# Block 0's second products as single fp32 matmuls, w_out's split parts made for block 1, and a dense slot for weight values

## The chip, the cores and the metric

One core of a Trainium2 chip. TensorE (PE) multiplies, VectorE (DVE), ScalarE (ACT) and GpSimd (POOL) work elementwise, and SyncE (SP) and the other engines issue DMAs. Each engine has its own queue of instructions in a fixed order, and waits on semaphores for the others. The metric is the device time of one execution in microseconds (us), the median of several runs.

## The reference, cut to what matters

Windowed attention, then a first MoE layer (512 to 2048 to 512) on 2304 tokens, then a second one with a softmax-like gate and a layer norm. The change touches the first MoE layer:

```python
def _moe_ref(x, w_in, w_out):
    h = x @ w_in
    g = np.where(h >= 1, h, np.where(h <= -1, 0.0, (h + 1) ** 2 / 4))
    return (g @ w_out).astype(np.float32)
```

The weights lie in memory as 64-bit floats. The result has to be close to that of fp32.

## The kernel before, in words

**Precision.** A product is made of three fp32r matmuls: an fp32 value is cut into a high part, which fp32r holds exactly, and the low rest, and the kernel adds high x high, high x low and low x high. `wih`/`wil` are the parts of w_in, `woh`/`wol` those of w_out, `xh`/`xl` those of the attention's output, `gh`/`gl` those of the activation g.

**Weights.** w_in and w_out come in 16 units of 512 KB each (a unit is one chunk f of 128 of the 2048 inner columns), w_in f and w_out f by turns. A unit lands as pairs of 32-bit words in a staging buffer `st` (`wst`, NST of them in a ring), SP issues the load (L124, L126). `split_a` on ACT (L132) and `split_b` on DVE (L136, L137) turn the pair into an fp32 value in place, every second word of the buffer; `split_c` casts it to the high part on ACT (L145) and subtracts on POOL for the low part (L146). The buffer is free for the next load after that subtraction.

**Blocks and chunks.** The tokens go in 6 blocks of 384. For each block the 16 chunks pass through: `moe_h` (L496), 4 x 3 matmuls into a PSUM bank `ps_h`, of which there are two in block 0; `moe_g`, ACT's Relu and Square (L505, L506); `moe_g2`, DVE's `u` (L511), which reads the bank a last time and so releases it, and ACT's cast `gh` (L512); `moe_g3`, the subtraction `gl` (L516), on POOL in block 0 and on DVE later; and, two steps on, `moe_y` (L527), 4 x 3 matmuls into the four accumulators `acc`. The first two chunks of block 0 are worked on in halves of 192 tokens, the rest in whole 384.

**What lies between.** Attention work for the next tokens runs in slots between the chunks (`ps_s`, L352, scores; `p`, L360 to L386, softmax; `ps_p`, L400 and L402, transposes; `pT`; `ps_x`, L421, values), all in plain fp32 on PE. In block 0 the weight units are loaded and split as well, two per chunk; from block 1 on the second layer's weights follow at a slower pace.

**Order.** The code is written in steps (the loop over `seq`), but a scheduler settles the order in each engine's queue, by its own estimate of when each instruction could start; it may bring an instruction far ahead of the step at which it is written.

Of the kernel before, what the change touches and what calls it, by code (L numbers as in the profile page):

```python
# [20 lines left out]
def kernel(  # L21
# [23 lines left out]
    NB = 384  # L45
    TPJ = NB // TT
    NBLK = NT // NB
    NF = DFF // 128
    KC = DM // 128
    NG = NTILES * NP  # L50
    NST = 5
    G0, F0, NC, NQ, NV = 6, 2, 4, 6, 7
    GB = TPJ * NP * 2
    PU = GB // 2 + 1
# [7 lines left out]
    gl_sb = const.tile([128, DF2 // 128], F32, name="gl_sb")  # L62
# [19 lines left out]
    wk_p = ctx.enter_context(tc.tile_pool(name="wk", bufs=2))  # L82
    w_p = ctx.enter_context(tc.tile_pool(name="w", bufs=1))
# [25 lines left out]
    def as_f32(a):  # L109
        return a.bitcast(F32)  # L110
# [7 lines left out]

    wdma = []

    def w_unit(src, hi, lo, gain=None, eng=nc.sync):
        st = stage["p"].tile([128, 512, 2], U32, tag="st", bufs=NST, name="wst")
        if src.shape[0] == 128 and len(src.shape) == 3:
            w_dma = eng.dma_start(out=st.rearrange("p (k f) t -> p k (f t)", k=src.shape[1]), in_=src)  # L124
        else:
            w_dma = eng.dma_start(out=st.rearrange("p f t -> p (f t)"), in_=src)  # L126
        wdma.append(w_dma.ins)
        return st, hi, lo, gain

    def split_a(st, *_):  # L130
        val = st[:, :, 1].bitcast(F32)
        nc.scalar.activation(val, val, ACTF.Prelu, scale=2.0 ** -112, alpha=2.0 ** 32)  # L132

    def split_b(st, *_):
        low, high = st[:, :, 0], st[:, :, 1]
        nc.vector.tensor_scalar(low, low, 29, None, op0=ALU.logical_shift_right)  # L136
        nc.vector.scalar_tensor_tensor(  # L137
            high, high, 3, low, op0=ALU.logical_shift_left, op1=ALU.bitwise_or
        )

    def split_c(st, hi, lo, gain):
        val = st[:, :, 1].bitcast(F32)
        if gain is not None:
            nc.scalar.activation(val, val, ACTF.Copy, scale=gain)
        nc.scalar.copy(hi, val)  # L145
        nc.gpsimd.tensor_tensor(lo, val, as_f32(hi), op=ALU.subtract)  # L146

    w_raw, w_a, w_b = [], [], []

    def w_conv(start=True):  # L150
        if w_b:
            split_c(*w_b.pop(0))
        if w_a:
            w_b.append(w_a.pop(0))
            split_b(*w_b[-1])
        if w_raw and start:
            w_a.append(w_raw.pop(0))
            split_a(*w_a[-1])

    wih, wil, woh, wol = {}, {}, {}, {}  # L160

    def wtile(tag):
        return w_p.tile([128, 512], F32R, tag=tag, name=tag)

    def w1_unit(f, which):
        if which == 0:
            hi, lo = wtile(f"wih{f}"), wtile(f"wil{f}")
            wih[f] = hi.rearrange("p (k f) -> p k f", k=KC)
            wil[f] = lo.rearrange("p (k f) -> p k f", k=KC)
            src = w_in[:, f * 256:(f + 1) * 256].rearrange("(k p) f -> p k f", p=128)  # L170
        else:
            hi, lo = woh[f], wol[f] = wtile(f"woh{f}"), wtile(f"wol{f}")
            src = w_out[f * 128:(f + 1) * 128, :]
        return w_unit(src, hi, lo)

# [6 lines left out]
    def w2_unit(n, which):  # L182
        if which == 0:
            kc, a = divmod(n, 2)
            src = w_in2[kc * 128:(kc + 1) * 128, a * 1024:(a + 1) * 1024]
            return w_unit(src, None, None, None, nc.gpsimd)
        src = w_out2.rearrange("(b k i) m -> k b i m", b=4, i=32)[n]
        return w_unit(src, None, None, gl_sb[:, n:n + 1], nc.gpsimd)

# [3 lines left out]
    w2_units = {}  # L193
    W2STEPS = [F0 + NF + 15 * u // 4 for u in range(16)]

    def w2_step(n, act, dve):
        for age, do in ((0, None), (4, split_a), (5, split_b), (6, split_c)):
            if n - age not in W2STEPS:
                continue
            u = W2STEPS.index(n - age)  # L200
            if age == 0:
                w2_units[u] = w2_unit(u % 8, u // 8)
                continue
            with tc.issue_after(act), tc.issue_after(dve):
                if age < 6:
                    do(*w2_units[u])
                    continue
                st, _, _, gain = w2_units.pop(u)
                if u < 8:
                    z = stage["p"].tile([128, 512], F32, tag="st", bufs=NST, name="w2st")  # L210
                    nc.scalar.copy(z, st[:, :, 1].bitcast(F32))
                    nc.gpsimd.dma_start(out=w2d[u], in_=z)
                    continue
                z = stage["p"].tile([128, 2, 512], F32R, tag="st", bufs=NST, name="w2st")
                do(st, z[:, 0, :], z[:, 1, :], gain)
                nc.gpsimd.dma_start(out=w2d[u], in_=as_f32(z.rearrange("p t f -> p (t f)")))
# [270 lines left out]
    hps, gh, gl, acc = {}, {}, {}, {}  # L487
# [12 lines left out]
    def moe_g(part, ps):  # L500
        c = part[2]
        u = wk_p.tile([128, NB], F32, tag="u", name="u")[:, c]
        hi = wk_p.tile([128, NB], F32R, tag="gh", bufs=3, name="gh")[:, c]
        lo = wk_p.tile([128, NB], F32R, tag="gl", bufs=3, name="gl")[:, c]
        nc.scalar.activation(u, ps, ACTF.Relu, bias=half, scale=0.5)  # L505
        nc.scalar.activation(u, u, ACTF.Square)  # L506
        gh[part[0], part[1], part[2].start], gl[part[0], part[1], part[2].start] = hi, lo
        return ps, u, hi, lo

    def moe_g2(ps, u, hi, lo):  # L510
        g = nc.vector.scalar_tensor_tensor(u, u, 1.0, ps, op0=ALU.min, op1=ALU.max)  # L511
# [205 lines left out]
    u = {}  # L717
# [122 lines left out]

    ps2 = []

    P_STEPS = {8: "P1", 9: "P6", 10: "P7", 12: "P5", 14: "P4"}

    na = 32 - 4 * G0
    seq = [(0, f, c) for c in (FIRST, SECOND) for f in range(F0)]
    seq += [(j, f, WHOLE) for j in range(NBLK) for f in range(F0 if j == 0 else 0, NF)]
    for n in range(len(seq) + 2):
        if n < len(seq):
            j, f, c = seq[n]  # L850
            last = j == NBLK - 1
# [133 lines left out]
```

## Time and profile before

| | |
|---|---|
| median of 3 runs | 712.16 us (713.34, 710.51, 712.16) |
| profiled execution, its own time | 712.67 us |
| its span | 710.9 us |
| granted clock, mean | 0.993 |
| busy: PE, DVE, ACT, POOL | 685.6, 434.3, 413.0, 195.3 us |
| DMA, mean rate over the span | 125 GB/s |

A busy time counts an instruction from its start to its modelled end; matmuls overlap, so PE's cost per matmul is read from one start to the next. Block 0's whole chunks run from about 52 to 139 us of the span, and POOL's work lies for the most part in the first fifth of it.

### The profile page before, as it was taken

Reading aid. Unit: us, or ns where it says so; the run is one execution under the profiler, and the core shown is the slowest. Engines: PE = TensorE matmul, PEld = TensorE weight load, DVE = VectorE, ACT = ScalarE, POOL = GpSimd, SP = SyncE. Lnnn points to the kernel's source line nnn. Section 1 sums busy time; section 2 is a strip of 40 time slices with the busy share of each in tenths; the row PEclk is TensorE's granted clock in tenths of the full one; section 3 lists DMA queues with packets and bytes.
Section 4 is the critical chain, followed back from the end, with each engine's and each line's share of the span. In section 5 each row is a group of like instructions: output and inputs, shape, how many; then the busy total and the mean of one; then the engine's idle time right before and its main releaser. Section 6 shows DMA issues by size and latency. Waiting matters only on the chain.

```text
span 710.9 us, 12663 instructions
## 1 busy us (share of the span) xinstructions
PE 685.6 (96%) x4439; PEld 630.0 (89%) x4439; DVE 434.3 (61%) x1147; ACT 413.0 (58%) x1006; POOL 195.3 (27%) x217
## 2 busy tenths in 40 slices
PE   6899978999999999999999999999999899999998
PEld 5689768999999999999999999999988678888887
DVE  4549898555555555454455543642379799988850
ACT  5778886565566655565566665454455635545541
POOL 2358876200001000021112111652472223300000
PEclk9989999999999999999999999999999999999999
DMA  9986897534353623346352211452033554553321
GB/s 193 216 231 171 220 260 189 107 81 107 71 110 88 139 61 73 78 124 130 87 112 70 95 60 47 154 200 89 1 126 97 175 164 155 175 177 122 131 74 45
DMA packets 155544, 88.94 MB, mean 125 GB/s; under 512 B 118616, under 2 KB 141400, under 8 KB 155480
## 3 DMA queue, kind: packets, MB, share of 16 engines
q1 hardware_dynamic: 144040, 64.00, 36.4%
q0 software_dynamic: 8704, 19.41, 8.4%
q10 hardware_dynamic: 2736, 4.72, 1.8%
q8 instruction: 35, 0.57, 0.4%
q14 instruction: 29, 0.24, 0.1%
HBM read 63.97 MB, written 24.12 MB: 124 GB/s over the span
## 4 chain that ended last, share of the span: by engine, by line
PE 72%; DVE 10%; issue 7%; POOL 4%; DMA 3%; ACT 2%; SPq 1%; DVEq 0%; POOLq 0%; ACTq 0%
PE ps_h L496 22%; PE acc L527 22%; PE ps_o L826 13%; PE P L711 7%; PE ps_x L476 2%; PE ps_p L402 2%; PE ps_s L442 2%; PE ps_s L352 2%; DVE wst L137 2%; POOL wil L249 2%; DVE wst L136 1%; PE ps_x L421 1%; DMA wst<-in_moe_w_out_dram 1%; DVE gl L516 1%; DVE s L740 1%
## 5 line engine op out<-in xcount | busy, mean ns | idle before, releaser
L511 DVE SCALAR_TENSOR_TENSOR u<-u,ps_h 128x384 f32<-128x384 f32 (+1 forms) x98 | 53.2, 543 | 143.8 <-ACT u L506 140.2
L496 PE MATMUL ps_h<-xh,wih 128*128 128x384 f32 (+1 forms) x392 | 132.6, 339 | 3.2 <-DVE u L511 3.1
L496 PE MATMUL ps_h<-xl,wih 128*128 128x384 f32 (+1 forms) x392 | 131.5, 336 | 1.4 <-DVE xl L429 1.4
L527 PE MATMUL acc<-gl,woh 128*128 128x384 f32 (+1 forms) x392 | 130.7, 335 | 2.2 <-DVE gl L516 1.3
L496 PE MATMUL ps_h<-xh,wil 128*128 128x384 f32 (+1 forms) x392 | 131.5, 336 | 0.0
L527 PE MATMUL acc<-gh,wol 128*128 128x384 f32 (+1 forms) x392 | 129.7, 333 | 0.0
L527 PE MATMUL acc<-gh,woh 128*128 128x384 f32 (+1 forms) x392 | 126.9, 342 | 0.0
L505 ACT ACTIVATE u<-ps_h,half 128x384 f32<-128x384 f32 (+1 forms) x98 | 55.9, 572 | 92.6 <-PE ps_h L496 92.4
L512 ACT CAST gh<-u 128x384 fp32r<-128x384 f32 (+1 forms) x98 | 49.7, 507 | 55.0 <-DVE u L511 37.8
L496 PEld LDWEIGHTS ps_h<-xh,wih 128*128 128x128 f32 x392 | 74.6, 190 | 5.2 <-DVE u L511 4.7
L527 PEld LDWEIGHTS acc<-gl,woh 128*128 128x128 f32 x392 | 73.8, 188 | 3.5 <-DVE gl L516 1.7
L496 PEld LDWEIGHTS ps_h<-xl,wih 128*128 128x128 f32 x392 | 74.7, 190 | 2.2 <-DVE xl L429 2.0
L516 DVE TENSOR_TENSOR gl<-u,gh 128x384 fp32r<-128x384 f32 x80 | 52.8, 661 | 37.3 <-ACT gh L512 36.7
L527 PEld LDWEIGHTS acc<-gh,woh 128*128 128x128 f32 x392 | 72.4, 188 | 3.0 <-issue 2.4
L496 PEld LDWEIGHTS ps_h<-xh,wil 128*128 128x128 f32 x392 | 74.7, 190 | 0.1
L527 PEld LDWEIGHTS acc<-gh,wol 128*128 128x128 f32 x392 | 73.7, 188 | 0.0
L711 PE MATMUL P<-wih,x2p 128*128 128x512 f32 x216 | 70.6, 391 | 0.5 <-DVE xo L539 0.5
L826 PE MATMUL ps_o<-woh,wol 128*128 128x512 f32 (+1 forms) x152 | 58.6, 385 | 2.9 <-DVE wol L814 2.9
L826 PE MATMUL ps_o<-woh,woh 128*128 128x512 f32 (+1 forms) x152 | 58.4, 384 | 0.0
L826 PE MATMUL ps_o<-wol,woh 128*128 128x512 f32 (+1 forms) x152 | 58.0, 382 | 0.0
L506 ACT ACTIVATE u<-u 128x384 f32<-128x384 f32 (+1 forms) x98 | 51.0, 521 | 2.0
L711 PEld LDWEIGHTS P<-wih,x2p 128*128 128x128 f32 x216 | 40.5, 188 | 9.2 <-DVE xo L539 0.9
(125 smaller groups left out, 1250.8 us busy)
## 6 DMA issues: line engine op xcount, KB each, us to landing
vw<-in_v_dram SPq DMA_DIRECT2D x32, 256.0 KB, 5.2
wst<-in_moe_w_in_dram SPq DMA_DIRECT2D x16, 512.0 KB, 5.2
wst<-in_moe_w_out_dram SPq DMA_DIRECT2D x16, 512.0 KB, 5.5
lnd<-e SPq DMA_DIRECT2D x16, 512.0 KB, 2.7
lT<-lnd SPq DMA_DIRECT2D x64, 128.0 KB, 3.0
x2d<-xo POOLq DMA_DIRECT2D x24, 192.0 KB, 2.5
out_dram<-o ACTq DMA_DIRECT2D x17, 256.0 KB, 2.9
wst<-in_moe_w_in_dram POOLq DMA_DIRECT2D x8, 512.0 KB, 5.3
```

Source lines behind the costliest of these rows:

```text
L137: nc.vector.scalar_tensor_tensor(high, high, 3, low, op0=ALU.logical_shift_left, op1=ALU.bitwise_or)
L249: nc.gpsimd.tensor_tensor(lo, v_, as_f32(hi), op=ALU.subtract)
L352: nc.tensor.matmul(ps[:, i * 128 + c0:i * 128 + 128], qT[g][:, i, :, :].rearrange("p x q -> p (x q)"), kT[g][:, i * 64 + c0:i * 64 + 128], ...
L496: nc.tensor.matmul(ps, a, bb[:, kc, c], start=(n == 0), stop=(n == 3 * KC - 1))
L505: nc.scalar.activation(u, ps, ACTF.Relu, bias=half, scale=0.5)
L506: nc.scalar.activation(u, u, ACTF.Square)
L511: g = nc.vector.scalar_tensor_tensor(u, u, 1.0, ps, op0=ALU.min, op1=ALU.max)
L512: return nc.scalar.copy(hi, u).ins, g.ins
L516: eng.tensor_tensor(lo, u, as_f32(hi), op=ALU.subtract)
L527: nc.tensor.matmul(acc[j, e][:, c], a, bb, start=(f == 0 and n == 0 and c.start == 0), stop=(f == NF - 1 and n == 2),)
L711: nc.tensor.matmul(ps, l, r, start=(n == 0), stop=(n == 5))
L826: nc.tensor.matmul(ps, a[kk // 4][:, kk % 4, :], b[kk][:, c:c + w], start=(n == 0), stop=(n == 3 * NK2 - 1),)
```

## The change

Four edits. In block 0 `moe_g2` writes the activation as one fp32 tile (`gh`, from DVE; no cast on ACT, no `gl`), and `moe_y` multiplies it with w_out's unsplit fp32 values `wov`: one fp32 matmul per accumulator in place of three fp32r ones. `wo_split`, at step 17 and after, makes `woh` and `wol` of these values for blocks 1 to 5. `split_b` writes its result into a dense tile of its own: for w_in `wiv`, in the slot that `woh` of that chunk takes later, for w_out `wov`, in the slot of the next chunk's `wol`; so a staging buffer is free after `split_b`. The ring has 4 buffers, not 5. The second layer's weights go as before.

```diff
-    NST = 5
+    NST = 4
...
-    def split_b(st, *_):
+    def split_b(st, val=None):
         low, high = st[:, :, 0], st[:, :, 1]
         nc.vector.tensor_scalar(low, low, 29, None, op0=ALU.logical_shift_right)
         nc.vector.scalar_tensor_tensor(
-            high, high, 3, low, op0=ALU.logical_shift_left, op1=ALU.bitwise_or
+            high if val is None else val.bitcast(U32), high, 3, low,
+            op0=ALU.logical_shift_left, op1=ALU.bitwise_or,
         )
...
-    def split_c(st, hi, lo, gain):
-        val = st[:, :, 1].bitcast(F32)
-        if gain is not None:
-            nc.scalar.activation(val, val, ACTF.Copy, scale=gain)
+    def split_c(val, hi, lo):
         nc.scalar.copy(hi, val)
         nc.gpsimd.tensor_tensor(lo, val, as_f32(hi), op=ALU.subtract)
...
         if w_a:
-            w_b.append(w_a.pop(0))
-            split_b(*w_b[-1])
+            st, val, hi, lo = w_a.pop(0)
+            split_b(st, val)
+            if hi is not None:
+                w_b.append((val, hi, lo))
...
         if which == 0:
-            hi, lo = wtile(f"wih{f}"), wtile(f"wil{f}")
+            val, hi, lo = w_p.tile([128, 512], F32, tag=f"woh{f}", name="wiv"), wtile(f"wih{f}"), wtile(f"wil{f}")
...
-        else:
-            hi, lo = woh[f], wol[f] = wtile(f"woh{f}"), wtile(f"wol{f}")
-            src = w_out[f * 128:(f + 1) * 128, :]
-        return w_unit(src, hi, lo)
+            return w_unit(src), val, hi, lo
+        val = wov[f] = w_p.tile([128, 512], F32, tag=f"wol{f + 1}", name="wov")
+        return w_unit(w_out[f * 128:(f + 1) * 128, :]), val, None, None
+
+    def wo_split(f):
+        woh[f], wol[f] = wtile(f"woh{f}"), wtile(f"wol{f}")
+        split_c(wov.pop(f), woh[f], wol[f])
...
     def moe_g2(ps, u, hi, lo):
+        if lo is None:
+            g = nc.vector.scalar_tensor_tensor(hi, u, 1.0, ps, op0=ALU.min, op1=ALU.max)
+            return None, g.ins
         g = nc.vector.scalar_tensor_tensor(u, u, 1.0, ps, op0=ALU.min, op1=ALU.max)
         return nc.scalar.copy(hi, u).ins, g.ins
 
-    def moe_g3(j, ps, u, hi, lo):
-        eng = nc.gpsimd if j == 0 else nc.vector
-        eng.tensor_tensor(lo, u, as_f32(hi), op=ALU.subtract)
+    def moe_g3(ps, u, hi, lo):
+        if lo is not None:
+            nc.vector.tensor_tensor(lo, u, as_f32(hi), op=ALU.subtract)
...
-            wh, wl = woh[f][:, e * 128:(e + 1) * 128], wol[f][:, e * 128:(e + 1) * 128]
-            for n, (a, bb) in enumerate(((wh, hi), (wh, lo), (wl, hi))):
+            if j == 0:
+                terms = [(wov[f][:, e * 128:(e + 1) * 128], hi)]
+            else:
+                wh, wl = (z[f][:, e * 128:(e + 1) * 128] for z in (woh, wol))
+                terms = [(wh, hi), (wh, lo), (wl, hi)]
...
+            if 0 <= n - WO < NF:
+                wo_split(n - WO)
```

PE's queue in the middle of block 0, before: one chunk's second product (`acc` from `gh`, `gl` and the parts of w_out), between two first products.

```order
L496 MATMUL ps_h<-xh,wil_857 128x384
L527 MATMUL acc_751<-gh,woh_787 128x384
L527 MATMUL acc_752<-gh,woh_787 128x384
L527 MATMUL acc_753<-gh,woh_787 128x384
L527 MATMUL acc_754<-gh,woh_787 128x384
L527 MATMUL acc_751<-gl,woh_787 128x384
L527 MATMUL acc_751<-gh,wol_788 128x384
L527 MATMUL acc_752<-gl,woh_787 128x384
L527 MATMUL acc_752<-gh,wol_788 128x384
L527 MATMUL acc_753<-gl,woh_787 128x384
L527 MATMUL acc_753<-gh,wol_788 128x384
L527 MATMUL acc_754<-gl,woh_787 128x384
```

The same place of the changed kernel (its line numbers are its own: L501 is the first product, L539 the second):

```order
L501 MATMUL ps_h<-xl,wih_1090 128x384
L501 MATMUL ps_h<-xh,wil_1091 128x384
L539 MATMUL acc_736<-gh,wov 128x384
L539 MATMUL acc_737<-gh,wov 128x384
L539 MATMUL acc_738<-gh,wov 128x384
L539 MATMUL acc_739<-gh,wov 128x384
```

Twelve instructions have become four, and the second product no longer comes in two parts around the wait for `gl`.

POOL's queue in block 0, before (`wil` and `wol` are the subtractions for the low parts of w_in and w_out, `p` a normalisation of the attention):

```order
L146 TENSOR_TENSOR wol_705<-wst,woh_704 128x512
L516 TENSOR_TENSOR gl<-u,gh 128x384
L146 TENSOR_TENSOR wil_709<-wst,wih_708 128x512
L146 TENSOR_TENSOR wol_788<-wst,woh_787 128x512
L386 TENSOR_TENSOR p<-p,rs 128x384
L516 TENSOR_TENSOR gl<-u,gh 128x384
L146 TENSOR_TENSOR wil_792<-wst,wih_791 128x512
L146 TENSOR_TENSOR wol_853<-wst,woh_852 128x512
L146 TENSOR_TENSOR wil_857<-wst,wih_856 128x512
L516 TENSOR_TENSOR gl<-u,gh 128x384
```

And in the changed kernel, about the same place:

```order
L391 TENSOR_TENSOR p<-p,rs 128x384
L144 TENSOR_TENSOR wil_883<-wiv,wih_882 128x512
L144 TENSOR_TENSOR wol_2043<-wov,woh_2042 128x512
L144 TENSOR_TENSOR wil_971<-wiv,wih_970 128x512
L144 TENSOR_TENSOR wol_2102<-wov,woh_2101 128x512
L144 TENSOR_TENSOR wil_1035<-wiv,wih_1034 128x512
L144 TENSOR_TENSOR wol_2145<-wov,woh_2144 128x512
L144 TENSOR_TENSOR wil_1091<-wiv,wih_1090 128x512
```

The `gl` rows are gone. The `wol` rows, written at block 1's steps, still stand among the `wil` rows of block 0; each belongs to a chunk some steps older than the `wil` beside it.

## Rows read from the trace of the kernel before

**Rows 1.** The page: PE's busy time, and the chain that ended last, by engine.
```profile
PE 685.6 (96%) x4439; PEld 630.0 (89%) x4439; DVE 434.3 (61%) x1147; ACT 413.0 (58%) x1006; POOL 195.3 (27%) x217
PE 72%; DVE 10%; issue 7%; POOL 4%; DMA 3%; ACT 2%; SPq 1%; DVEq 0%; POOLq 0%; ACTq 0%
```
**Rows 2.** Windows of block 0's whole chunks and their middle; columns in the first line.
```profile
core 0: us, PE busy (x) PEld busy (x) DVE busy (x) ACT busy (x) POOL busy (x), PEclk, DMA share, GB/s
52.40:139.00 86.60, 78.67 (x528) 72.32 (x525) 75.04 (x174) 66.07 (x170) 59.59 (x47) 1.00 0.77 191
61.30:103.90 42.60, 37.89 (x248) 33.82 (x248) 39.82 (x86) 34.60 (x84) 35.08 (x26) 1.00 0.89 229
```
**Rows 3.** Timeline of PE in block 1: start, length, instruction.
```profile
251.28 0.33 PE L496 MATMUL ps_h<-xh,wih 128*128 128x384 f32 x1
...
253.18 0.34 PE L496 MATMUL ps_h<-xh,wil 128*128 128x384 f32 x1
```
**Rows 4.** Groups of PE, 52.4 to 139: count, busy us, mean ns, idle before.
```profile
L496 PE MATMUL ps_h<-xh,wih 128*128 128x384 f32 x57 | 20.2, 354 | 3.2 <-DVE u L511 3.1
L527 PE MATMUL acc<-gl,woh 128*128 128x384 f32 x56 | 19.6, 350 | 0.9 <-POOL gl L516 0.9
...
L352 PE MATMUL ps_s<-kq 128*128 128x128 f32 x40 | 6.0, 281 | 0.0
```
**Rows 5.** Waits, 52.4 to 139: us in total, times, longest.
```profile
ACT gh L512 <- DVE u L511: 5.0, 7, 1.1
...
PE ps_h L496 <- DVE u L511: 3.1, 5, 1.3
PE ps_p L400 <- DVE p L382: 2.8, 2, 1.7
...
DVE wst L136 <- DMA wst<-in_moe_w_out_dram: 2.4, 3, 1.5
```
**Rows 6.** Timeline of one chunk of block 0, PE, ACT and DVE.
```profile
68.56 0.33 PE L496 MATMUL ps_h<-xh,wil 128*128 128x384 f32 x1
...
72.77 0.57 ACT L505 ACTIVATE u<-ps_h,half 128x384 f32<-128x384 f32 x1
...
77.11 0.52 DVE L511 SCALAR_TENSOR_TENSOR u<-u,ps_h 128x384 f32<-128x384 f32 x1
...
77.68 0.45 PE L496 MATMUL ps_h<-xh,wih 128*128 128x384 f32 x1
```
**Rows 7.** Groups of DVE, 52.4 to 139.
```profile
L137 DVE SCALAR_TENSOR_TENSOR wst<-wst 128x512 uint32<-128x512 uint32 x25 | 28.9, 1165 | 0.6 <-ACT wst L132 0.4
L136 DVE TENSOR_SCALAR wst<-wst 128x512 uint32<-128x512 uint32 x24 | 19.4, 809 | 2.4 <-DMA wst<-in_moe_w_out_dram 2.4
```
**Rows 8.** The same groups, 140 to 450.
```profile
L137 DVE SCALAR_TENSOR_TENSOR wst<-wst 128x512 uint32<-128x512 uint32 x16 | 11.0, 690 | 0.4
...
L136 DVE TENSOR_SCALAR wst<-wst 128x512 uint32<-128x512 uint32 x16 | 6.8, 422 | 0.0
```
**Rows 9.** Timeline: six records of fp32 matmuls in block 0.
```profile
71.15 0.83 PE L352 MATMUL ps_s<-kq 128*128 128x128 f32 x6
```
**Rows 10.** Timeline of PE in the second layer, products of 512 columns.
```profile
639.71 0.39 PE L826 MATMUL ps_o<-woh,wol 128*128 128x512 f32 x1
...
642.43 0.39 PE L826 MATMUL ps_o<-woh,wol 128*128 128x512 f32 x1
```
**Rows 11.** Groups of POOL, 52.4 to 139.
```profile
L146 POOL TENSOR_TENSOR wol<-wst,woh 128x512 fp32r<-128x512 f32 x13 | 20.2, 1550 | 6.5 <-ACT woh L145 6.5
...
L516 POOL TENSOR_TENSOR gl<-u,gh 128x384 fp32r<-128x384 f32 x14 | 16.4, 1169 | 10.1 <-ACT gh L512 10.0
```
**Rows 12.** Timeline of one staging buffer: load, DVE, POOL, the load that follows in it.
```profile
73.77 0.38 SPq L124 DMA_DIRECT2D wst<-in_moe_w_in_dram  x1
...
81.73 1.81 DVE L137 SCALAR_TENSOR_TENSOR wst<-wst 128x512 uint32<-128x512 uint32 x1
...
84.66 1.50 POOL L146 TENSOR_TENSOR wil<-wst,wih 128x512 fp32r<-128x512 f32 x1
...
86.80 0.39 SPq L126 DMA_DIRECT2D wst<-in_moe_w_out_dram  x1
```

More of the change, by code (lines that the diff above doesn't have):

```diff
@@ L119, with w_unit @@
     wdma = []
-    def w_unit(src, hi, lo, gain=None, eng=nc.sync):
+    def w_unit(src, eng=nc.sync):
         st = stage["p"].tile([128, 512, 2], U32, tag="st", bufs=NST, name="wst")
@@ L127, in w_unit, with split_a @@
         wdma.append(w_dma.ins)
-        return st, hi, lo, gain
-    def split_a(st, *_):
+        return st
+    def split_a(st):
         val = st[:, :, 1].bitcast(F32)
         nc.scalar.activation(val, val, ACTF.Prelu, scale=2.0 ** -112, alpha=2.0 ** 32)
-    def split_b(st, *_):
+    def split_b(st, val=None):
         low, high = st[:, :, 0], st[:, :, 1]
@@ L153, in w_conv @@
         if w_a:
-            w_b.append(w_a.pop(0))
-            split_b(*w_b[-1])
+            st, val, hi, lo = w_a.pop(0)
+            split_b(st, val)
+            if hi is not None:
+                w_b.append((val, hi, lo))
         if w_raw and start:
             w_a.append(w_raw.pop(0))
-            split_a(*w_a[-1])
-    wih, wil, woh, wol = {}, {}, {}, {}
+            split_a(w_a[-1][0])
+    wih, wil, woh, wol, wov = {}, {}, {}, {}, {}
     def wtile(tag):
@@ L185, in w2_unit @@
             src = w_in2[kc * 128:(kc + 1) * 128, a * 1024:(a + 1) * 1024]
-            return w_unit(src, None, None, None, nc.gpsimd)
+            return w_unit(src, nc.gpsimd), None
         src = w_out2.rearrange("(b k i) m -> k b i m", b=4, i=32)[n]
-        return w_unit(src, None, None, gl_sb[:, n:n + 1], nc.gpsimd)
+        return w_unit(src, nc.gpsimd), gl_sb[:, n:n + 1]
     w2_units = {}
@@ L196, in w2_step @@
     def w2_step(n, act, dve):
-        for age, do in ((0, None), (4, split_a), (5, split_b), (6, split_c)):
+        for age, do in ((0, None), (4, split_a), (5, split_b), (6, None)):
             if n - age not in W2STEPS:
@@ L205, in w2_step @@
                 if age < 6:
-                    do(*w2_units[u])
+                    do(w2_units[u][0])
                     continue
-                st, _, _, gain = w2_units.pop(u)
+                st, gain = w2_units.pop(u)
+                val = st[:, :, 1].bitcast(F32)
                 if u < 8:
                     z = stage["p"].tile([128, 512], F32, tag="st", bufs=NST, name="w2st")
-                    nc.scalar.copy(z, st[:, :, 1].bitcast(F32))
+                    nc.scalar.copy(z, val)
                     nc.gpsimd.dma_start(out=w2d[u], in_=z)
@@ L214, in w2_step @@
                 z = stage["p"].tile([128, 2, 512], F32R, tag="st", bufs=NST, name="w2st")
-                do(st, z[:, 0, :], z[:, 1, :], gain)
+                nc.scalar.activation(val, val, ACTF.Copy, scale=gain)
+                split_c(val, z[:, 0, :], z[:, 1, :])
                 nc.gpsimd.dma_start(out=w2d[u], in_=as_f32(z.rearrange("p t f -> p (t f)")))
@@ L502, in moe_g @@
         u = wk_p.tile([128, NB], F32, tag="u", name="u")[:, c]
-        hi = wk_p.tile([128, NB], F32R, tag="gh", bufs=3, name="gh")[:, c]
-        lo = wk_p.tile([128, NB], F32R, tag="gl", bufs=3, name="gl")[:, c]
+        hi = wk_p.tile([128, NB], F32R if part[0] else F32, tag="gh", bufs=3, name="gh")[:, c]
+        lo = wk_p.tile([128, NB], F32R, tag="gl", bufs=3, name="gl")[:, c] if part[0] else None
         nc.scalar.activation(u, ps, ACTF.Relu, bias=half, scale=0.5)
@@ L524, in moe_y @@
         for e in range(KC):
-            wh, wl = woh[f][:, e * 128:(e + 1) * 128], wol[f][:, e * 128:(e + 1) * 128]
-            for n, (a, bb) in enumerate(((wh, hi), (wh, lo), (wl, hi))):
+            if j == 0:
[3 more added lines that the diff above has]
+                terms = [(wh, hi), (wh, lo), (wl, hi)]
+            for n, (a, bb) in enumerate(terms):
                 nc.tensor.matmul(
                     acc[j, e][:, c], a, bb,
-                    start=(f == 0 and n == 0 and c.start == 0), stop=(f == NF - 1 and n == 2),
+                    start=(f == 0 and n == 0 and c.start == 0), stop=(f == NF - 1 and n == len(terms) - 1),
                 )
@@ L841 @@
     ps2 = []
+    WO = F0 + NF - 1
     P_STEPS = {8: "P1", 9: "P6", 10: "P7", 12: "P5", 14: "P4"}
@@ L876 @@
         if n >= 1 and n - 1 < len(seq):
-            moe_g3(seq[n - 1][0], *prev)
+            moe_g3(*prev)
         if n < len(seq):
```

## The prediction, on record before the changed kernel ran

> **What bounds the kernel now.** I read the page first: PE is busy for 685.6 of 710.9 us and the chain that ended last runs over PE for 72% of the span [rows 1]. So a change pays only where PE stands still, or by shortening PE's own work. The instruction orders of the two kernels are the same on every engine from the middle of block 1 on, so whatever happens, happens before about 145 us. I took the windows of the stretch in which block 0's whole chunks 2 to 15 run, 52.4 to 139.0 us [rows 2]: 86.6 us for 14 chunks, 6.19 us a chunk. Here three other engines are loaded too: DVE 75.0, ACT 66.1, POOL 59.6 us.
>
> PE's "busy" overlaps, so I priced its instructions by start-to-start spacing. Twelve products in a row start from 251.28 to 253.18, 0.173 us each for 384 columns [rows 3]. The groups of the stretch hold 57+56 (wih) +56 (wil) +3x56 (second product) = 337 of these (groups that repeat one of those shown have 56, one of them with some records missing) [rows 4]: 337x0.1735 = 58.5 us. For the 24 halves I allow 0.11 each, 2.6. The attention's fp32 pieces I put at about 11, an estimate: 0.111 a record of 128 columns (below) for the 40 of L352 [rows 4] and as many again of other transposes and products, and about 2 us of smaller ones. Sum 72; the stretch takes 86.6, so **14.6 us are lost**. The list of waits names 6.8 of them: 3.1 for a PSUM bank of the first product that DVE's u (L511) releases, 2.8 for the attention's normalised p, 0.9 for gl [rows 4, 5]. The other 7.8 are waits too short for that list and gaps at changes of work.
>
> How the bank wait comes about is seen on one chunk [rows 6]: its first product ends at 68.89, ACT takes it at 72.77, 3.9 us late because of conversion work queued ahead, DVE finishes u at 77.63 behind transposes and reductions, and PE starts the product after next at 77.68, in the same bank (there are two). Here PE itself stood still for only some tenths; elsewhere for up to 1.3 us [rows 5]. DVE itself is slow there: L137 and L136 mean 1165 and 809 ns in this stretch [rows 7], 690 and 422 ns where POOL is nearly idle [rows 8]. (25x0.475)+(24x0.387) = 21 us of DVE's 75 are stretched that way, beside POOL's 59.6 us.
>
> **The change, part by part.**
>
> *Second product of block 0.* Per chunk and e, three fp32r matmuls (3x0.1735 = 0.52) give way to one fp32 matmul. No fp32 matmul with 384 columns is in the trace. What is there: fp32 with 128 columns, six records for three matmuls in 0.83 us, so (0.83-0.28)/5 = 0.111 a record, two records a matmul [rows 9, 4]; and fp32r with 512 columns every 0.227 us (12 spacings from 639.71 to 642.43, [rows 10]), so 128 columns more cost 0.227-0.1735 = 0.0535 a pass. 0.111 is two such passes and 0.004, so a record makes two passes, and with 384 columns it takes 2x3x0.0535+0.004 = 0.325; the matmul 0.65. Bounds: each record costs one fp32r spacing, 0.347; or each matmul is four such spacings, 0.694. Per e that is +0.13 (bounds -0.173, +0.173); over 14x4 = 56 of them **+7.2 us** (-9.7, +9.7). I take 7.2 since 128 columns already cost two passes a record. The halves cost about the same either way (3x0.11 against half of 0.65).
>
> The Trainium skill ("FP8 and Floating Point Precision", section "TensorE Precision Notes") says that true fp32 takes four passes, which the 0.111 us bears out, and its page "TensorE: Matmul & The Clock Gate" (section "Back-to-back issue gap") gives N/2.4+2.5 ns for one isolated matmul; together they would make four 162.5 against three 162.5 ns, +9.1 us, a rule that speaks against the change. The row has 173.5 ns where that rule has 162.5, so I stay with the rows.
>
> *ACT's gh cast and POOL's gl in block 0* vanish. With gh go 5.0 us in which ACT stood waiting for u [rows 5]; with gl 16.4 us of POOL for the whole chunks [rows 11], and its waiting for gh, in which the weights' subtractions behind it waited too. DVE's u writes gh directly: same instruction, no new cost. The second product then waits for DVE instead of DVE, ACT and POOL. PE's 0.9 for gl goes entirely.
>
> *w_out's parts.* The code makes them at block 1's steps, but the order shows that the scheduler puts eleven of the POOL subtractions and their ACT casts back among block 0's wil, and the last five right behind. So of 13 wol in the stretch (20.2 us, [rows 11]) only some five leave, 7.5 us. Each hoisted wol waits for a second product two or more chunks old, since its slot held the next-lower chunk's values; behind it stands a wil needed several chunks later. I cost that at nothing while PE's order keeps that distance; without the cover it is one subtraction, 1.5 us, per chunk hit. POOL thus falls from 59.6 to about 35 us (59.6-16.4-7.5); if DVE's stretching falls in proportion (21x24/59.6), DVE is lighter by about 8 us, or 0.6 a chunk.
>
> *Dense slot, ring of four.* A staging buffer now comes free at the end of DVE's L137, not of POOL's subtraction. For one unit [rows 12]: issued at 73.77, L137 ends 83.54, POOL 86.16, buffer reloaded at 86.80. Five buffers at 13.03 us are 2.61 a unit; four at 83.54-73.77+0.64 = 10.41 are 2.60. A chunk needs two, 5.2 us, below PE's 6.19 either way: no term. Ahead of chunk 2 the fifth load now comes later, but its values are needed only at 52; I allow 0 (bounds -0.8, +0.8; the idle PE time there is for attention data).
>
> *What PE gets back.* PE's queue between the end of one first product and the reuse of its bank now holds two second products, each 4x0.13 = 0.52 longer. At unchanged u the five bank waits (3.1 us, the longest 1.3) shrink by up to 1.04 each; with the lighter DVE and ACT they go but for about 0.5: -2.6. The p waits (2 times; DVE's and POOL's queues ahead of the normalisation) I put at half to all of 2.8, -2.0. gl -0.9. Of the unnamed 7.8 I take -0.8 (bounds 0 and -2.4). Sum: 7.2-2.6-2.0-0.9-0.8 = **+0.9 us**.
>
> The profiled execution took 712.67, 0.5 above the median of the three runs, 712.16. So 712.67+0.9 = 713.6 for it, and on the runs' scale **713.1 us**. What a measurement of this kernel can tell from no change is about 0.5%, 3.6 us: below 708.6 is faster, above 715.7 slower.
>
> **The rivals.**
>
> *A (forecast, 0.57): a draw.* PE's added passes fill its own waits; 710.0 to 715.6.
>
> *B (0.18): the gaps are not waits for what is removed.* The hoisted wol keep POOL and DVE colliding (L137 stays near 1.1 us), u stays equally late relative to PE, since the loop simply turns with PE; only gl's 0.9 goes. 712.16+7.2-0.9 = 718.5. Against it: at a fixed chain, a longer PE queue must eat bank waits. It decides once less than 3.6 us of the 14.6 come back.
>
> *C (0.10): the ring of four binds.* Its cycle need only grow from 10.41 to above 12.9 us for a chunk to take 2x12.9/4 = 6.44 us, 14x0.25 = 3.6 us in all. For it: DMA is already busy for 0.89 in the middle [rows 2], DVE waits 2.4 us for w_out units [rows 5], and L137, which now frees the buffer, took 1.81 us there [rows 12]. Against it: DVE gets lighter. At 13.3 the time is 712.2+14x0.46 = 718.6.
>
> *D (0.13): more comes back.* All 6.8 named waits and 2.4 of the others go, and chunk 2 starts 0.8 earlier (ACT and POOL lighter): 7.2-6.8-2.4-0.8 = -2.8, 709.4; with fp32 cheaper too, say 0.60 a matmul, 56x0.05 = 2.8 less, 706.6. Of this case half is below 708.6. *The cheap end of fp32* (0.02) would give 712.2-9.7-0.9 = 701.6.
>
> *That the splits don't really move to block 1* is certain from the order and is in the forecast; if they left wholly (all 20.2 us) D would be likelier.
>
> **How the numbers follow.** Time 713.1, from A. B and C and a tail of A's bounds (fp32 at 0.694, 2.5 us more) lie above, D below: **709.0 to 718.3** leaves out one in ten on either side; A alone is 710.0 to 715.6. Slower by over 0.5%: B and C's 0.28, less a little of C that stays short of its point, 0.27. Faster: half of D, the cheap end, and 0.04 for what I haven't seen, 0.13. The rest, 0.60.
>
> **What would show it.** In the profile after: the second product as records of 128x384 fp32, two a matmul, start-to-start about 0.325; PE's list with the wait on u near 0.5 and none on gl; L137 and L136 nearer to 0.9 and 0.65 us; POOL about 35 us busy in block 0; the distance from chunk 2's start to block 1's start 87 to 88 us; and everything behind block 1's first chunks moved by that alone. A stretch above 90 us with unchanged waits on u says B; with waits of DVE on DMA, C; a record spacing away from 0.325 mis-sizes the first term.

## The result

The changed kernel takes 715.11 us in the median of 20 runs (711.15 to 717.88), the kernel before 711.12 us (709.69 to 714.09, 20 runs): a ratio of 1.0051, 95% interval 1.0033 to 1.0068. That is 3.6 us more (2.3 to 4.8), at the edge of what I called no change, and 2.0 us above the forecast of 713.1. The profiled execution took 715.06 us, its span is 713.1. Medians and ratios leave out two runs that were far longer than the rest, 757.7 us of the kernel before and 969.27 us of one experiment.

**The new product costs what was worked out.** Timeline of PE in the changed kernel (start, length, instruction; the second product is now L539):

```profile
93.78 2.74 PE L539 MATMUL acc<-gh,wov 128*128 128x384 f32 x8
96.83 0.44 PE L501 MATMUL ps_h<-xh,wih 128*128 128x384 f32 x1 [0.30 <-DVE gh L517]
```

Four matmuls are eight records. Each is 0.485 us long in the trace, so the seven spacings are (2.74-0.485)/7 = 0.322 us each: 0.645 a matmul, where 0.65 was forecast. Against three fp32r at 0.5205 that is 0.1245, and 56 of them make +7.0 us.

**PE's waits changed their kind.** Waits of PE in block 0's whole chunks, 51.3 to 144.6 us, to be read beside [rows 4, 5]:

```profile
PE ps_p L405 <- DVE p L387: 2.0, 1, 2.0
PE ps_x L426 <- ACT pT L412: 1.3, 2, 1.0
PE ps_p L407 <- POOL p L391: 1.2, 1, 1.2
PE ps_p L407 <- DVE p L391: 0.9, 1, 0.9
PE ps_h L501 <- DVE gh L517: 0.3, 1, 0.3
```

The wait for a bank of the first product fell from 3.1 to 0.3, that for gl is gone; but the waits for the softmax's p are 4.1 (2.0, 1.2 and 0.9) where they were 2.8, and that for its transpose `pT` is 1.3 where it was 0.8.

**Where in block 0.** The starts of chunks 2, 8, 12 and of block 1 cut the stretch in three. Windows of the kernel before (columns as in [rows 2]):

```profile
52.40:84.10 31.70, 29.55 (x201) 27.25 (x198) 29.98 (x65) 27.42 (x68) 25.67 (x20) 1.00 0.74 199
84.10:110.40 26.30, 21.66 (x139) 19.34 (x139) 25.04 (x51) 20.57 (x50) 20.23 (x16) 1.00 0.98 248
110.40:139.00 28.60, 27.46 (x191) 25.73 (x190) 20.03 (x60) 18.09 (x54) 13.69 (x13) 1.00 0.61 129
```

and of the changed kernel:

```profile
51.30:85.20 33.90, 31.62 (x187) 25.90 (x187) 28.99 (x67) 27.41 (x68) 21.34 (x16) 0.97 0.68 190
85.20:114.20 29.00, 25.51 (x124) 18.68 (x123) 21.99 (x52) 18.30 (x45) 13.29 (x11) 0.88 0.96 265
114.20:144.60 30.40, 30.40 (x167) 22.58 (x165) 13.70 (x48) 13.45 (x42) 10.33 (x9) 1.00 0.44 87
...
100.00:108.00 8.00, 6.42 (x18) 4.50 (x19) 7.49 (x18) 5.19 (x11) 4.19 (x4) 0.57 1.01 220
```

Chunks 2 to 7 take 2.2 us more, 8 to 11 2.7 more, 12 to 15 1.8 more: 93.3 against 86.6, less 1.1 by which chunk 2 starts earlier. In the last part PE is busy without a gap: there the passes bind. The middle part holds what the forecast did not have, waits and a stretch at half clock: with 0.88 on the mean, 7 of its 29.0 us ran at the lower level. Its worst place is near 100 us, in the timeline of DVE, POOL and PE:

```profile
97.98 0.43 DVE L136 TENSOR_SCALAR wst<-wst 128x512 uint32<-128x512 uint32 x1 [0.53 <-DMA wst<-in_moe_w_out_dram]
...
99.24 1.27 POOL L144 TENSOR_TENSOR wil<-wiv,wih 128x512 fp32r<-128x512 f32 x1 [4.28 <-ACT wih L143]
99.31 1.29 DVE L387 TENSOR_TENSOR p<-p,rs 128x64 f32<-128x64 f32 x1
100.48 1.27 POOL L144 TENSOR_TENSOR wol<-wov,woh 128x512 fp32r<-128x512 f32 x1
100.52 1.51 DVE L391 TENSOR_TENSOR p<-p,rs 128x256 f32<-128x256 f32 x1
100.65 0.30 PE L405 MATMUL ps_p<-ident,p 128*64 128x128 f32 x1 [1.99 <-DVE p L387]
```

DVE waits for a late weight unit, then its two normalisations of p take 1.29 and 1.51 us, each beside one of POOL's subtractions: the first beside a `wil`, which the kernel before makes as well, the second beside a hoisted split of w_out (the smaller of the two takes 0.22 us on the mean of block 1 on). PE stands for 1.99 us, and then for 0.93 more. From 101 to 107.7 us the granted clock is at 0.5, the lower of its two levels.

DVE's and POOL's groups in the same stretch (count, busy us, mean ns, idle before):

```profile
L136 DVE TENSOR_SCALAR wst<-wst 128x512 uint32<-128x512 uint32 x24 | 15.7, 657 | 5.0 <-DMA wst<-in_moe_w_out_dram 4.6 <-DMA wst<-in_moe_w_in_dram 0.3
L137 DVE SCALAR_TENSOR_TENSOR wiv<-wst 128x512 uint32<-128x512 uint32 x12 | 11.2, 930 | 3.9 <-ACT wst L132 3.4
L137 DVE SCALAR_TENSOR_TENSOR wov<-wst 128x512 uint32<-128x512 uint32 x13 | 9.5, 728 | 1.1 <-ACT wst L132 0.9
...
L391 DVE TENSOR_TENSOR p<-p,rs 128x256 f32<-128x256 f32 x4 | 2.8, 690 | 0.0
```

```profile
L144 POOL TENSOR_TENSOR wol<-wov,woh 128x512 fp32r<-128x512 f32 x15 | 20.4, 1363 | 18.7 <-PE acc L539 14.5 <-PE ps_p L405 3.4 <-PE ps_p L407 0.8
L144 POOL TENSOR_TENSOR wil<-wiv,wih 128x512 fp32r<-128x512 f32 x13 | 19.5, 1499 | 19.9 <-ACT wih L143 19.9
```

L137 and L136 came down as forecast (0.83 on the mean and 0.66 us, from [rows 7]), but for L137 the lighter POOL is only part of the reason. With the dense slots alone and POOL as busy as before (the first experiment below, 52 to 140 us) they are

```profile
L136 DVE TENSOR_SCALAR wst<-wst 128x512 uint32<-128x512 uint32 x25 | 20.1, 807 | 2.6 <-DMA wst<-in_moe_w_out_dram 1.7 <-DMA wst<-in_moe_w_in_dram 0.9
L137 DVE SCALAR_TENSOR_TENSOR wiv<-wst 128x512 uint32<-128x512 uint32 x13 | 12.8, 987 | 0.2
L137 DVE SCALAR_TENSOR_TENSOR wov<-wst 128x512 uint32<-128x512 uint32 x13 | 12.5, 964 | 0.0
```

so some 0.19 of L137's 0.34 us come with the staging, and L136's whole fall with the rest. POOL still makes 15 wol in the stretch, as much work as the 13 of before [rows 11], and only gl's is gone. DVE's waits for weight units rose from 2.4 [rows 5] to 4.9 us.

Behind block 1's second chunk the profiled execution runs 5.9 us late, almost without change, to 540 us; by 576 us it is 1.7, by the end 2.2. The kernel before loses the difference in its own profile: PE stands there for the second layer's `wol`, and from 570.8 to 574.2 the clock is at half.

```profile
569.27 0.50 PE L826 MATMUL ps_o<-woh,wol 128*128 128x512 f32 x1 [2.17 <-DVE wol L814]
```

None of the other profiles has a half clock there, so the ends of two profiles are not compared below, only their block 0.

### The profile page after: what moved, and what is told of

It is laid out like the page before. It is cut to its first block, busy times and chain, and to the rows that moved or that the text cites. A ratio compares the mean times of both kernels' runs of the same rounds, so it can differ in the third digit from the quotient of the medians.

```text
span 713.1 us, 12437 instructions
## 1 busy us (share of the span) xinstructions
PE 690.3 (97%) x4367; PEld 621.3 (87%) x4367; DVE 424.3 (60%) x1147; ACT 405.3 (57%) x988; POOL 175.1 (25%) x199
## 4 chain that ended last, share of the span: by engine, by line
PE 81%; DVE 7%; ACT 5%; DMA 3%; issue 2%; POOL 1%; SPq 1%; DVEq 0%; POOLq 0%; ACTq 0%
PE acc L539 26%; PE ps_h L501 25%; PE ps_o L838 13%; PE P L723 9%; PE ps_x L481 2%; PE ps_p L407 2%; PE ps_s L357 2%; PE ps_s L447 2%; ACT p L371 2%; DMA qk<-in_q_dram 1%; DMA wst<-in_moe_w_out_dram 1%; DVE gl L524 1%; PE ps_x L426 1%; DVE wiv L137 1%; DVE s L752 1%
## 5 line engine op out<-in xcount | busy, mean ns | idle before, releaser
L501 PE MATMUL ps_h<-xh,wih 128*128 128x384 f32 (+1 forms) x392 | 134.4, 343 | 0.4 <-DVE gh L517 0.3
L501 PE MATMUL ps_h<-xl,wih 128*128 128x384 f32 (+1 forms) x392 | 131.6, 336 | 0.6 <-DVE xl L434 0.5
L501 PE MATMUL ps_h<-xh,wil 128*128 128x384 f32 (+1 forms) x392 | 131.5, 336 | 0.0
L519 DVE SCALAR_TENSOR_TENSOR u<-u,ps_h 128x384 f32<-128x384 f32 x80 | 44.3, 554 | 140.5 <-ACT u L511 139.5
L539 PE MATMUL acc<-gh,woh 128*128 128x384 f32 x320 | 108.5, 344 | 0.0
L539 PE MATMUL acc<-gl,woh 128*128 128x384 f32 x320 | 107.1, 335 | 1.3 <-DVE gl L524 1.3
L539 PE MATMUL acc<-gh,wol 128*128 128x384 f32 x320 | 106.6, 335 | 0.0
L501 PEld LDWEIGHTS ps_h<-xh,wih 128*128 128x128 f32 x392 | 74.4, 190 | 2.6 <-DVE gh L517 0.9
L501 PEld LDWEIGHTS ps_h<-xl,wih 128*128 128x128 f32 x392 | 74.7, 191 | 1.9 <-DVE xl L434 0.9
L501 PEld LDWEIGHTS ps_h<-xh,wil 128*128 128x128 f32 x392 | 74.5, 190 | 0.2
L520 ACT CAST gh<-u 128x384 fp32r<-128x384 f32 x80 | 41.1, 514 | 49.4 <-DVE u L519 32.4
L539 PEld LDWEIGHTS acc<-gh,woh 128*128 128x128 f32 x320 | 60.0, 188 | 2.8 <-issue 2.6
L539 PEld LDWEIGHTS acc<-gl,woh 128*128 128x128 f32 x320 | 60.1, 188 | 1.7 <-DVE gl L524 1.7
L539 PEld LDWEIGHTS acc<-gh,wol 128*128 128x128 f32 x320 | 60.0, 188 | 0.1
```

The lines of the kernel that those rows point to most:

```text
L501: nc.tensor.matmul(ps, a, bb[:, kc, c], start=(n == 0), stop=(n == 3 * KC - 1))
L539: nc.tensor.matmul(acc[j, e][:, c], a, bb, start=(f == 0 and n == 0 and c.start == 0), stop=(f == NF - 1 and n == len(terms) - 1),)
```

## The experiments

Twelve runs in three batches and a last one; each batch shares the runs of the kernel before. Every ratio is to these, with its 95% interval; the changed kernel itself was not run again beside them.

**The two halves of the change.** The staging alone: the changed kernel's slots and ring under the old product.

```diff
-    NST = 5
+    NST = 4
...
+            return w_unit(src, [val, lambda: (hi, lo)], None)
...
+        def parts():
+            woh[f], wol[f] = wtile(f"woh{f}"), wtile(f"wol{f}")
+            return woh[f], wol[f]
```

Expected: 

> Only the dense slots and the ring of 4; the second product of block 0 is three fp32r matmuls again, gh and gl as before, w_out split at once. Theory 1 (the added fp32 passes on PE make the difference, the ring of 4 is as fast as that of 5): 710 to 713 us, near the 711.1 of before, DVE's wait for units' DMA near before's 2.4 us in block 0. Rival (the ring of 4 brings the units late): 714 us or more without any fp32 product, with DVE and ACT waiting for DMA as in the changed kernel (4.6 and 10.2 us).

Measured: 710.83 us, 0.9995 (0.9975 to 1.0014). DVE's wait for units' DMA is 2.6 us in its block 0. The ring of 4 and the dense slots cost nothing and bring nothing in time, to within some 1.5 us.

The product alone: ring of 5, w_in in its staging buffer.

```diff
-            return w_unit(src), val, hi, lo
+            return w_unit(src), None, hi, lo
...
-    NST = 4
+    NST = 5
```

Expected: 

> Only the fp32 product (with w_out's values in dense slots and its parts made later); ring of 5, w_in split in its staging buffer and freed by POOL as before; the accumulators' copies share the slots of gl to make room. Theory 1: 713 to 717 us as with the whole change. Rival (ring of 4): 709 to 712 us, since gh and gl are gone and the ring is the old one.

Measured: 714.56 us, 1.0060 (1.0039 to 1.0081). The whole difference is in the product and what goes with it (gh, gl, later splits).

**How much PE's passes count.** Half of the columns:

```diff
             if j == 0:
+                if c == WHOLE:
+                    c, hi = FIRST, hi[:, FIRST]
```

Expected: 

> The changed kernel, but block 0's whole chunks multiply only the first 192 of 384 columns in the second product, so that part of the output is left out: PE has 56 x 0.32 = 18 us less to do. Theory 1 (PE's work binds in block 0): 700 to 706 us. Rival (units' arrival and the chain over ACT and DVE bind, PE only follows): 711 us or more.

Measured: 702.35 us, 0.9896 (0.9870 to 0.9923). Against the changed kernel's 1.0051 that is 11.0 us by the ratios (12.8 by the medians) for 18.1 us of PE. PE's work binds, but 0.3 to 0.4 of each microsecond is not seen in the time.

**The hoisted splits.** They are held behind ACT's Square:

```diff
             if 0 <= n - WO < NF:
-                wo_split(n - WO)
+                with tc.issue_after(sq[-1]):
+                    wo_split(n - WO)
```

Expected: 

> The changed kernel with w_out's splits held back on ACT until the Square of the step at which they are written, so that none stands in block 0. Theory 1 (POOL's subtractions in block 0 cost nothing now): 714 to 717 us, block 0 within 1 us of the changed kernel's. Rival (the hoisted splits stretch DVE's L136 and L137 and sit ahead of wil): block 0 3 us shorter, 711 to 713 us, with L137 near 0.8 us instead of 1.0.

Measured: 713.25 us, 1.0026 (1.0008 to 1.0045). Chunk 2 to block 1 takes 90.8 us in its profile, 2.5 less than in the changed kernel, and DVE's conversions take less in all (52 to 139 us: 32.8 us, of 36.4), though `wov`'s are longer:

```profile
L136 DVE TENSOR_SCALAR wst<-wst 128x512 uint32<-128x512 uint32 x24 | 12.8, 536 | 11.3 <-DMA wst<-in_moe_w_out_dram 6.2 <-DMA wst<-in_moe_w_in_dram 5.0
L137 DVE SCALAR_TENSOR_TENSOR wov<-wst 128x512 uint32<-128x512 uint32 x13 | 11.2, 861 | 2.6 <-ACT wst L132 2.6
L137 DVE SCALAR_TENSOR_TENSOR wiv<-wst 128x512 uint32<-128x512 uint32 x12 | 8.8, 737 | 1.7 <-ACT wst L132 1.3
```

That POOL's subtractions stretch DVE, the rival's mechanism, is so; that this costs time is not shown. The time lies between the two expectations, and its interval overlaps the changed kernel's. The 2.5 us may be the clock's alone: here chunks 2 to 7 and 8 to 11 have a clock of 0.97 and 1.00, where the changed kernel has 0.97 and 0.88, some 7 us more at half.

```profile
52.60:83.30 30.70, 30.70 (x183) 25.49 (x183) 26.47 (x67) 22.73 (x57) 11.56 (x9) 0.97 0.72 204
83.30:112.90 29.60, 23.52 (x127) 17.32 (x126) 18.75 (x52) 16.72 (x42) 8.70 (x7) 1.00 0.85 227
```

And PE's waits hardly moved (51 to 145 us; the 1.2 ends before chunk 2 starts):

```profile
PE ps_p L405 <- DVE p L387: 3.0, 2, 1.9
PE ps_x L426 <- ACT pT L412: 2.2, 1, 2.2
PE ps_p L407 <- POOL p L391: 1.2, 1, 1.2
```

In the stretch 3.0 us for p are left, of 4.1, the longest again for a normalisation of 1.29 us, here beside a `wil`; the wait for `pT` grew from 1.3 to 2.2. DVE spends what it gains waiting for units: 11.2 us on DMA.

**Which chunks pay.** Two hybrids with the new staging: fp32 for chunks 0 to 7 or for 8 to 15, three fp32r matmuls with gh and gl for the others.

```diff
+    def fp32(j, f):
+        return j == 0 and f < FH
...
-            if j == 0:
+            if fp32(j, f):
```

(f >= FH in the second; FH = 8.) Expected of the first: 

> fp32 second products only for chunks 0 to 7 of block 0; chunks 8 to 15 with three fp32r matmuls, gh, gl on POOL and w_out split at once as before (w_out 15 in its staging buffer). Theory 1 (PE's waits cover the added passes in the early chunks, where PE stood waiting before, and not in the late ones): 710 to 712.5 us. Rival (each chunk pays the same share of the 4 us): 713 us.

Measured: 712.78 us, 1.0032 (1.0009 to 1.0055). Expected of the second: 

> The other way round: three fp32r matmuls for chunks 0 to 7, fp32 for 8 to 15. Theory 1: 713.5 to 716 us, the late chunks pay 8 x 0.5 us in full. Rival (same share for each chunk): 713 us.

Measured: 708.44 us, 0.9980 (0.9964 to 0.9996). Both theories are wrong here: the late chunks pay nothing, the early ones about 2 us, and the two intervals lie apart. The parts don't add up to the whole: +2.3 and -1.4 us where the whole change has +3.6. Windows of the staging alone, cut at the same chunks:

```profile
52.00:85.50 33.50, 29.51 (x204) 27.88 (x203) 31.68 (x69) 28.64 (x73) 24.65 (x19) 0.95 0.68 192
85.50:114.20 28.70, 24.64 (x167) 22.05 (x166) 25.65 (x59) 21.48 (x58) 21.85 (x18) 1.00 0.86 231
114.20:140.20 26.00, 25.67 (x172) 24.54 (x171) 18.23 (x49) 15.72 (x46) 13.42 (x13) 1.00 0.67 141
```

of fp32 in the late chunks, whose windows up to chunk 7 are nearly the same but for the clock:

```profile
51.10:85.30 34.20, 30.12 (x203) 28.52 (x203) 32.05 (x69) 29.44 (x74) 25.34 (x20) 0.90 0.67 189
85.30:110.50 25.20, 24.32 (x157) 20.51 (x156) 21.50 (x58) 19.81 (x52) 13.44 (x10) 1.00 0.97 254
110.50:139.00 28.50, 28.50 (x150) 21.37 (x148) 17.41 (x52) 14.65 (x44) 12.28 (x11) 1.00 0.64 136
```

and of fp32 in the early ones:

```profile
51.40:86.30 34.90, 30.85 (x185) 25.13 (x186) 29.50 (x68) 27.86 (x69) 22.48 (x17) 1.00 0.70 194
86.30:116.40 30.10, 25.51 (x139) 21.39 (x138) 26.88 (x54) 20.47 (x48) 21.31 (x17) 0.90 0.95 249
116.40:143.40 27.00, 27.00 (x185) 25.61 (x185) 14.93 (x53) 15.85 (x49) 9.22 (x10) 0.98 0.46 90
```

With fp32 late, chunks 8 to 11 shrink from 28.7 to 25.2 us and POOL's work in them from 21.9 to 13.4; PE's list of waits no longer has the normalised p, though 3.0 us for a bank stay. Chunks 12 to 15 grow by 2.5, where PE has no gap left. Over the whole block the profile is level with that of the kernel before: block 1 starts at 139.0 us in both, with some 7 us at half clock on the way in this one and none in that one. So that fp32 in the late chunks gains on the kernel before inside block 0 is not shown. With fp32 early, chunks 8 to 11 take 30.1: PE waits there and before for p,

```profile
PE ps_p L423 <- POOL p L407: 3.2, 1, 3.2
PE ps_p L421 <- DVE p L403: 3.0, 2, 2.7
...
PE ps_p L423 <- DVE p L407: 1.0, 1, 1.0
```

7.2 us (51 to 145 us), against 3.1 in the staging alone.

**SP's queue.** In the changed kernel, SP issues 14 attention loads in a row between two weight loads (75.8 to 84.0 us; the expectation below says 16), and the next unit reaches DVE 2.6 us late; before, and with the product's early chunks left as they were, the longest such rows are of nine and eight. That made a second theory: the order on SP, not the passes, costs the 4 us. First two rough tries, each attention load behind the weights written ahead of it, and the weights on POOL's queue:

```diff
+        pin = wdma[-1]
...
+                    with tc.issue_after(pin):
+                        nc.sync.dma_start(out=a[p0:p0 + 32, m0:m0 + n // 32, :], in_=s_[e])
```

Expected: 

> The changed kernel, but on SP each attention load stands behind the weight loads that the code writes ahead of it. Theory 1 (PE's passes are the cost, late units matter little): 714 to 717 us. Rival (the runs of eight and more attention loads on SP ahead of the weights starve DVE and ACT, whose waits for DMA rose): 711 to 713 us, DVE's and ACT's waits for weight DMA halved.

Measured: 717.83 us, 1.0088 (1.0065 to 1.0111).

```diff
-            return w_unit(src), val, hi, lo
+            return w_unit(src, nc.gpsimd if f > 3 else nc.sync), val, hi, lo
```

Expected: 

> The changed kernel with the weight loads of chunks 4 to 15 issued by POOL, so that no attention load stands ahead of them; each costs POOL about 0.65 us. Theory 1: 714 to 717 us. Rival (SP's queue makes the units late): 711 to 713 us.

Measured: 718.76 us, 1.0116 (1.0095 to 1.0137). Neither tells the theories apart: the first put 32 attention loads in a row and left DVE's waits for DMA at 8.6 us; in the second DVE's list has no wait for a weight unit any more, but each load takes 0.6 to 0.8 us of POOL. So the order was fixed by hand, four attention loads after each weight load, then two:

```diff
             if wq:
-                w_raw.append(w1_unit(*wq.pop(0)))
+                with tc.issue_after(wdma[-1]) if wdma else ExitStack():
+                    w_raw.append(w1_unit(*wq.pop(0)))
+            for _ in range(4):
+                if qpend:
+                    with tc.issue_after(wdma[-1]):
+                        qpend.pop(0)[1]()
```

Expected: 

> The changed kernel with SP's order in block 0 fixed by hand: after each weight load at most four attention loads (the traces of before, of the staging alone and of the fp32 product in late chunks alone have one to five there, with one run of eight; the changed kernel has a run of 16). Theory 2 (the added passes are covered also in the early chunks, and the 4 us come from units that are late behind attention loads on SP, so that DVE, and with it the softmax's p, is late): 708 to 712 us, the waits of PE for p halved, DVE's for weight DMA below 3 us. Theory 1 (the passes cost 4 us): 714 to 717 us.

Measured: 715.19 us, 1.0056 (1.0034 to 1.0079). In the profile DVE's waits for weight DMA fall to 2.8 us and those of PE for p to 2.1, chunk 2 to block 1 takes 88.4 us, but chunk 2 starts at 54.3, 3 us late, and PE's wait for a bank is back at 2.7. So theory 2's two signs came and its time did not, with the late start as a possible reason.

Expected of two: 

> The same with two attention loads after each weight load; the attention's loads then lag. Theory 2: as with four, 708 to 712 us, unless the attention's loads become late themselves. Theory 1: 714 to 717 us.

Measured: 720.94 us, 1.0137 (1.0103 to 1.0171); now DVE waits 14.8 us for attention loads. Last, four between, with the first group's loads where they were:

```diff
-                    if wq:
+                    if wq and g > NPE:
```

Expected: 

> As with four attention loads after each weight load, but the eight loads for the first group of pairs stay where the changed kernel has them, ahead of chunk 2, since in the run with four the stretch from chunk 2 to block 1 was 4.9 us shorter (88.4 against 93.3) and chunk 2 began 3 us later. Theory 2 (order on SP): chunk 2 begins near 51.5, the stretch takes 88 to 90, 710 to 712.5 us. Theory 1 (the passes): 714 us or more.

Measured: 714.17 us, 1.0037 (1.0019 to 1.0056). Chunk 2 starts at 51.4 as wanted and chunks 8 to 11 shrink, but the time comes back ahead of them:

```profile
51.40:88.40 37.00, 31.43 (x185) 25.05 (x185) 33.87 (x73) 30.76 (x73) 23.34 (x17) 0.97 0.73 221
88.40:112.50 24.10, 24.06 (x122) 18.94 (x123) 17.27 (x47) 15.27 (x39) 11.17 (x9) 0.90 0.92 227
```

Chunks 2 to 7 take 37.0 us where the changed kernel has 33.9, the whole stretch 91.5, and DVE's waits for weight DMA are back at 5.7. No order on SP that was tried reached the second theory's range; the last is 1.0 us below the changed kernel by the ratios, with overlapping intervals (from 0.8 more to 2.8 less), so the runs can't tell it from nothing.

**A better version.** fp32 in the late chunks is the one kernel with the whole output that is below the kernel before, by 0.2%, its interval just clear of 1. With twelve intervals of 95%, one so close may be chance. With its splits held back:

```diff
+                with tc.issue_after(sq[-1]):
+                    wo_split(n - WO)
```

Expected: 

> fp32 second products for chunks 8 to 15 alone, as in the run that came out below the kernel before, and their w_out splits held back on ACT until the steps of block 1. If the held splits give the 2 us that they gave the whole change: 706 to 708 us; if they only mattered with POOL's 16 of them in the early chunks: 708 to 709 us, no change to that run.

Measured: 710.00 us, 0.9988 (0.9967 to 1.0009), no better; and no longer clear of the kernel before.

## Why the prediction was right in range and low by 2 us

*Luck in the number*: the forecast change was +0.9 us, the measured one +3.6. The time came out only 2.0 too low because the +0.9 stood on 712.16 us, the median of three runs; 20 runs of the kernel before give 711.12.

*The price of the product* (+7.2): 7.0 by the records. Right.

*PE's bank waits and gl* (-2.6 and -0.9): 3.1 went to 0.3 and 0.9 to nothing. Right. That refutes rival B's bank wait that turns with PE, and its 718.5 is outside the interval; but by its measure the case was close, 3.4 us came back where B was to decide under 3.6, and its other half, POOL and DVE still in each other's way, is what the normalisations at 100 us show.

*The waits for p* (-2.0): the step that failed. They rose by 1.3 instead, to 4.1. I had put them down to DVE's and POOL's queues, which were to get lighter. "Only some five leave, 7.5 us" and with it POOL at 35 us were wrong: 15 wol stood in the stretch and not 8, and POOL has 42.5 between 52 and 139 us. Beside POOL's subtractions two normalisations of p took 1.29 and 1.51 us; by what they take alone (0.22 and 0.42) that makes an estimated 2.0 of the 4.1, 1.07 of the wait of 1.99 and the 0.93. The hoisted splits are not the whole of it: held back, the 128x256 normalisation went from 690 to 418 ns, but 3.0 us for p stayed, 1.9 of them behind a normalisation beside a `wil`, and `pT` took up 0.9. Nor is the stretched normalisation enough by itself: in the staging alone that of 128x256 has 689 ns, with 2.0 us for p in the stretch and no loss of time. What made p late in the rest stays open.

*The unnamed gaps* (-0.8) and *the start* (0): chunk 2 starts 1.1 us earlier in the profile, a little beyond its bound of 0.8. The gaps can't be read apart from the clock, for which the sum had no term: up to half of the 8.6 us that the stretch ran at half level. Of the 7.8 that I called unnamed, 1.2 stood in the list of waits after all (0.8 for `pT`, 0.4 for `xl`).

*The ring of 4, rival C*: no term, as forecast. By the prediction's own signs the profile spoke for C, with 93.3 us where 87 to 88 were named and DVE's waits on DMA at 4.9; the staging alone, with the ring of 4 and no loss, and the product alone, with the ring of 5 and the whole loss, decide against it.

*The balance*: the passes' 7.0 us less the 3.6 measured leave 3.4 us that came back, where 6.3 were forecast. The half columns fit: a microsecond of PE less is worth 0.6 to 0.7 here. If it costs as much to add one, which no run shows, 7 of them cost 4 to 5, and the lighter DVE, ACT and POOL gave back about one. The forecast's picture, all of PE's waits as room for its passes, counted waits for p as room too; they come when they come, and a later PE meets the next one.

*Where it would have paid*: I thought that waits in the early chunks were the room, and the experiments put it the other way round. In the profiles the relief shows in chunks 8 to 11, where PE's gaps went from 4.1 to 0.9 us, though DVE, ACT and POOL are as busy in the chunks ahead of them. Why fp32 in the early chunks makes p later, in the kernels alike that have it, stays open: every one of these kernels has another static order on five queues, one profile each shows where the waits fell and not why. The order on SP was the one candidate that was tried, and no order brought the time back.

## What to carry to other kernels

A wait of the bounding engine is room for more of its work only if the waited-for thing would have come at the same time; count a wait for another chain as a wait, not as room, unless the change shortens that chain. Try a change on half of the chunks at a time: half of this one beat the whole of it, and the half that I would have picked was the wrong one. Before two stretches of two profiles are compared, compare their clocks. A step that is written later may be scheduled earlier: count in the order, not in the code, how much really leaves a stretch, and hold it back on the first engine of its chain if it must.

## What the runs showed of the hardware

In the changed kernel's profile PE was busy for 0.66 of the 2 us from 98 on, and for 0.35 and 0.25 of the next two single ones; from 101 the clock was at half, and it was still there at 106 with PE busy without a gap:

```profile
98.00:100.00 2.00, 0.66 (x4) 0.34 (x2) 1.79 (x4) 1.46 (x4) 0.76 (x1) 1.00 1.10 319
100.00:101.00 1.00, 0.35 (x2) 0.22 (x2) 1.00 (x2) 1.00 (x3) 1.00 (x2) 0.93 0.83 149
101.00:102.00 1.00, 0.25 (x1) 0.00 (x0) 1.00 (x2) 1.00 (x4) 0.75 (x1) 0.50 0.56 85
...
106.00:107.00 1.00, 1.00 (x3) 0.51 (x2) 0.90 (x3) 0.20 (x1) 0.00 (x0) 0.50 1.37 231
107.00:108.00 1.00, 1.00 (x3) 0.53 (x2) 0.99 (x9) 0.92 (x2) 0.63 (x1) 0.66 1.12 277
```

So by an estimate from these rows waits of some 3 us cost up to 3.3 more, half of the 6.7 us at the lower level. It explains much of this one profile's middle part, but not the medians: the mean granted clock of the changed kernel's 20 runs is 0.991, that of 27 runs of the kernel before 0.992, about 1.5 us more at half clock on the mean, and so less than 1 us of time.

The normalisation of 128x64 values took 1.29 us beside a POOL subtraction of 1.27. The Trainium skill ("SBUF — State Buffer", section "SBUF: two separate sides") says that DVE operations with two SBUF inputs and GpSimd share a port pair that one of them holds for a whole instruction; the trace agrees: 1.29 beside 1.27, and 1.51 beside 1.27 for an operation that takes 0.42 alone, each ending 0.1 to 0.3 us after the subtraction beside it.

L136, a DVE operation with one input, is longer too where POOL is busier: on the mean it takes 807 ns with POOL busy for 59.9 us of block 0's whole chunks (staging alone), 657 with 45.0 (the changed kernel), 536 with 24.5 (splits held) and 422 where POOL is nearly idle [rows 8].
